# A recurrent memory layer on Trainium2: the query and key images of every segment transposed by DMA instead of on TensorE

## The chip, the cores and the metric

The kernel runs on one core of a Trainium2 chip. The core has a matrix engine (TensorE, PE), three engines that work on vectors (VectorE or DVE, ScalarE or ACT, GpSimd or POOL), and SyncE (SP), which in this kernel only issues DMA transfers. The engines run in parallel, each through its own list of instructions in order, and wait for each other by semaphores. The metric is the device time of one execution in microseconds (us), as the median of the runs shown.

## The reference

The model has four layers with a residual connection around each: A, B, A, B. Layer A is attention over segments of 32 rows with a recurrent memory of 8 rows; layer B is linear attention. The change touches layer A alone. Cut to what matters:

```python
x = x + A(layernorm(x)); x = x + B(layernorm(x)); x = x + A(layernorm(x)); x = x + B(layernorm(x))

def A(x, mem0, Wq, Wk, Wv, Wo, seg_len):          # x 2048x512, 64 segments of 32 rows, memory 8x512
    for s in range(64):
        h = concat(mem, x[32*s : 32*s+32])        # 40 rows
        q, k, v = h @ Wq, h @ Wk, h @ Wv          # 32 heads of 128
        p = softmax(mask(q @ k.T * 128**-0.5))    # memory columns are open, the rest is causal
        o = (p @ v) @ Wo                          # 40 x 512
        mem = o[:8]                               # the next segment's memory
        outs.append(o[8:])
    return concat(outs)
```

All weights and activations are bfloat16. The memory makes the 64 segments of a layer a recurrence: a segment's projections can't start until the output projection of the segment before has given the 8 memory rows.

## The kernel before

Each segment has 40 rows, but the kernel's matrix tiles take 32. Rows 0 to 31 of a segment (8 memory rows and 24 of its own) make its block; the 8 rows left over from each of four segments are put together into a left-over block of 32 rows per group of four segments (`prepare` and `left_block`, lines 671 to 706). The left-over block doesn't depend on the memory, and its projections are made ahead of time.

A projection (`project`, line 633) holds the 32 rows as weights in one of four column tiles of TensorE (`tile_position=(0, 32 * j)`) and streams 512 columns of Wq, Wk or Wv; four tiles j work side by side, so that a PSUM bank gets heads 8j + 4b to 8j + 4b + 3 of half b in its partitions 32j to 32j+31. That takes 16 products of 512 columns. A segment needs six: query and key for half 0, query and key for half 1, and the values for both halves (lines 888 to 895).

The scores need the query and key with the 128 elements of a head on the partitions, so the bank is copied to SBUF as a bfloat16 "image" of 128 x 512 (line 650, done by ScalarE or VectorE through the helper `evac`, lines 516 and 517) and then transposed. This is done in two ways before the change. `transposed` (lines 645 to 660) does it for a segment's own block: four 128 x 128 transposes on TensorE into PSUM (line 655), and a second copy from there to `qT` or `kT` (line 658). `turned` (lines 662 to 669) does it for the left-over block: one DMA transpose, issued by SP, from the image straight to its place (line 668).

With these, `mem_attention` (line 708) attends for the 8 memory rows: a bias product (717), scores (725), exponential (732), sums (737), reciprocal by logarithm and exponential (740, 742), values (750, 751) and the multiplication into `oTb` (754). `out_block` (832) does the output projection (823), and `next_mem` (836) picks the 8 rows out of it (842) and puts them into the next segment's block. `x_attention` (759) attends for the segment's other 32 rows, 24 of its block and 8 left over: lines 768 to 776 first copy the left-over query columns next to the segment's own, then multiply 32 columns of queries by each head's keys (774), again on four column tiles. Its values are at 807 and 808. Its result goes into the output projection of the next segment, so it isn't on the recurrence. `residual` (851) adds the outputs to x.

The order of the instructions is made by a planner (`_Prog.schedule`, lines 125 to 313). It is a list scheduler: every operation has a cost, written at its `add`; the longest path behind it gives its priority; and it is appended to its engine's list when the engine is free and its inputs are done. The cost of a DMA issue is 0.1 us on SP, and `lat` is the time from there to landing. Each engine then runs its list in this fixed order, whatever the real times are. `urgent` operations, those on the recurrence, may take the last PSUM banks. PE has two modes, `col` with four column tiles and `full`, and the planner groups work by mode. SP's list has the DMA transposes in the order of their planned starts, and an issue that waits for its image holds up those behind it.

Of the kernel before, what the change touches and what calls it, by code (L numbers as in the profile page):

```python
# [33 lines left out]
def c_pe(n_mm, n):  # L34
    return n_mm * max(0.0255, (n / 2.4 + 3.0) * 1e-3)
# [364 lines left out]
def _build_kernel(nc, A_x, A_mem0, A_Wq, A_Wk, A_Wv, A_Wo, A_seg_len, B_wqkv, B_wo, out):  # L400
# [11 lines left out]
    ANY = ("act", "dve")  # L412
# [54 lines left out]
    img = av((NI + 2) * 512).rearrange("p (r x) -> p r x", r=NI + 2)  # L467
    vimg = av(2 * 1024).rearrange("p (r x) -> p r x", r=2)
    vleft = av(2 * 1024).rearrange("p (r x) -> p r x", r=2)
    qT = av(2 * 1280).rearrange("p (r h j x) -> p r h j x", r=2, h=8, j=4)  # L470
    kT = av(2 * 1024).rearrange("p (r h j x) -> p r h j x", r=2, h=8, j=4)
    qTl = av(2 * 1024).rearrange("p (r h j x) -> p r h j x", r=2, h=8, j=4)
    kTl = av(2 * 1024).rearrange("p (r h j x) -> p r h j x", r=2, h=8, j=4)
# [155 lines left out]
    def a_layer(layer):  # L629
# [12 lines left out]
                add("pe", mm, c_pe4(4, 512), reads=[key] + bkeys, tiles=[tl], urgent=urgent, mode="col")  # L642
            return tl

        def transposed(W, key, blk, bkeys, b, dst, dkey, urgent):

            tl = project(W, key, blk, bkeys, b, urgent)
            k = img_no[0] % NI if urgent else NI + img_no[1] % 2
            img_no[0 if urgent else 1] += 1
            nd = evac(img[:, k, :], lambda: tl.f32()[:, :], 512, tiles=[tl], writes=[("img", k)], urgent=urgent)  # L650
            tt = P.tile()

            def tr(pe):
                for i in range(4):
                    r = pe.transpose(tt.bf16()[:, 128 * i:128 * i + 128], img[:, k, 128 * i:128 * i + 128], id_sb[:, :])  # L655
                return r
            add("pe", tr, c_pe(4, 128), reads=[("img", k), "id"], tiles=[tt], urgent=urgent)
            evac(dst, lambda: tt.bf16()[:, 0:512].rearrange("p (h j x) -> p h j x", h=4, j=4), 512, tiles=[tt],
                 writes=[dkey], rate=2, urgent=urgent)
            return nd  # L660

        def turned(W, key, blk, bkeys, b, dst, dkey):

            tl = project(W, key, blk, bkeys, b, False)
            k = NI + img_no[1] % 2
            img_no[1] += 1
            evac(img[:, k, :], lambda: tl.f32()[:, :], 512, tiles=[tl], writes=[("img", k)])
            add("sp", lambda e: e.dma_start_transpose(dst.rearrange("p h j x -> p h (j x)"), img[:, k, :]), 0.1,
                reads=[("img", k)], writes=[dkey], dsem="turn%d" % k, lat=3.0)

        def left_block(G):
            r2 = G % 2
# [86 lines left out]
        def x_attention(s):  # L759

            G, g = divmod(s, 4)
            r2, g2 = s % 2, G % 2
            s1 = (s + 1) % 3
            gl = slice(8 * g, 8 * g + 8)
            tl = P.tile()
            for b in range(2):
                hs = slice(4 * b, 4 * b + 4)
                add(ANY, copy(qT[:, r2, hs, :, 32:40], qTl[:, g2, hs, :, gl]),
                    {"act": c_act(128, 0, 1), "dve": c_dve(128)}, reads=[("qTl", g2, b)], writes=[("qTL", r2, b)])

                def mm(pe, b=b):
                    for hh in range(4 * b, 4 * b + 4):
                        for j in range(4):
                            r = pe.matmul(tl.f32()[32 * j:32 * j + 32, 32 * hh:32 * hh + 32], kT[:, r2, hh, j, :],  # L774
                                          qT[:, r2, hh, j, 8:40], start=True, stop=True, tile_position=(0, 32 * j))
                    return r
                add("pe", mm, c_pe4(16, 32), reads=[("kT", r2, b), ("qT", r2, b), ("qTL", r2, b)], tiles=[tl], mode="col")
            add("act", lambda a: a.activation(Px[:, :, :].rearrange("p h q -> p (h q)"), tl.f32()[:, 0:256], ACTF.Exp,  # L778
                                              scale=SCALE), c_act(256), tiles=[tl], writes=["Px"])
            add("dve", lambda v: v.tensor_tensor(Px[:, :, :], Px[:, :, :],  # L780
                                                 mx_sb[:, :].unsqueeze(1).to_broadcast([128, 8, 32]), ALU.mult),
                c_dve(256, 2), reads=["Px", "mx"], writes=["Px"])

            def sums(pe):
                o = tl.f32()[:, 256:512].rearrange("p (h q) -> p h q", h=8)
                pe.matmul(o, bo_sb[:, :], Px[:, :, :], start=True, stop=False)
                return pe.matmul(o[:, :, 24:32], bo_sb[:, :], PLL[:, g2, :, gl], start=False, stop=True)
            add("pe", sums, c_pe(1, 256) + c_pe(1, 64), reads=["Px", ("PLL", g2), "bo"], tiles=[tl])
            add("act", lambda a: a.activation(Rx[:, :, :].rearrange("p h q -> p (h q)"), tl.f32()[:, 256:512], ACTF.Ln),
                c_act(256), tiles=[tl], writes=["Rx"])  # L790
            add("act", lambda a: a.activation(Rx[:, :, :], Rx[:, :, :], ACTF.Exp, scale=-1.0), c_act(256, 0, 1),  # L791
                reads=["Rx"], writes=["Rx"])
            for j in range(4):
                q = slice(32 * j, 32 * j + 32)
                add("dve", lambda v, q=q, j=j: v.tensor_tensor(Pbx[q, :, j, 0:32], Px[q, :, :], Rx[q, :, :], ALU.mult),  # L795
                    c_dve(256), reads=["Px", "Rx"], writes=[("Pbx", j)])
                add("dve", lambda v, q=q, j=j: v.tensor_tensor(Pbx[q, :, j, 32:40], PLL[q, g2, :, gl], Rx[q, :, 24:32],  # L797
                                                               ALU.mult),
                    c_dve(64), reads=[("PLL", g2), "Rx"], writes=[("Pbx", j)])
            for b in range(2):  # L800
                pv = P.tile()
                for i in range(4):
                    def pvx(pe, i=i, b=b, pv=pv):
                        hh = 4 * b + i
                        o = pv.f32()[:, 128 * i:128 * i + 128].rearrange("p (j q) -> p j q", j=4)
                        e = slice(128 * hh, 128 * hh + 128)
                        pe.matmul(o, vimg[:, r2, e], Pbx[:, hh, :, 0:32], start=True, stop=False)  # L807
# [74 lines left out]
        for s in range(NSEG):  # L882
            G, g = divmod(s, 4)
            r2 = s % 2
            blk = hT[:, G % 2, g, :, :]
            bk = [("hTm", G % 2, g), ("hTx", G % 2, g)]
            early = []
            for b in range(2):
                hs = slice(4 * b, 4 * b + 4)
                transposed(Wq_sb, "Wq", blk, bk, b, qT[:, r2, hs, :, 0:32], ("qT", r2, b), True)  # L890
                early.append(transposed(Wk_sb, "Wk", blk, bk, b, kT[:, r2, hs, :, :], ("kT", r2, b), True))
            for b in range(2):
                tl = project(Wv_sb, "Wv", blk, bk, b, True)
# [174 lines left out]
```

## Time and profile before

| | before |
|---|---|
| median of 3 runs | 2032.45 us (2032.11 to 2033.56) |
| the profiled execution's own time | 2032.45 us |
| its span, first to last instruction | 2030.7 us |
| PE, ACT, DVE busy | 1946.7, 1274.8, 1015.3 us |
| granted clock of TensorE, mean | 0.988 |
| first memory layer's stretch, 63 to 935 us: PE busy | 864.46 of 872.00 us |
| second memory layer's stretch, 1070 to 1940 us: PE busy | 861.35 of 870.00 us |
| DMA transposes | 128, median 2.5 us from issue to landing |

The profile is one execution, recorded by the hardware. Busy time is the time in which an engine worked on an instruction; for PE it comes from modelled ends of pipelined products, so that "busy" isn't "at its peak". The chain of work that ended last is followed back from the last instruction, at each step to what released it, and tells which engine and line the time goes to. A group of instructions has a line number of the kernel; the copies of the helper `evac` all have its lines (516 on ACT, 517 on DVE) and are told apart by their shapes. Rows in order of time have the start, the duration, the engine, the line, what is written and read, and a count; what stands in brackets is the engine's idle time ahead of it and what ended it. "SPq" is SP's queue of DMA issues; its duration is the time for which the issue holds SP, and the landing is when the transfer's semaphore has its full count.

### The profile page before, as it was taken

What the parts mean: (1) busy time and instruction counts of PE and PEld (TensorE: products, weight loads), DVE (VectorE), ACT (ScalarE), POOL (GpSimd) and SP (SyncE); (2) the same over time, 40 slices, a digit from 0 to 9 for tenths busy, and PEclk for the clock granted to TensorE, in tenths of its full rate; (3) what the DMA queues carried; (4) which work ended last, traced back from release to release, by engine and by line L of the source; (5) the groups of instructions that cost most, each with busy time, mean ns of one, the idle gap of its engine ahead of it and who ended that gap; (6) DMA issues with size and microseconds to landing.
All of it is one profiled execution on the core that took longest, in us unless ns stands there. A gap on an engine that the chain in (4) does not pass through costs nothing.

```text
span 2030.7 us, 81374 instructions
## 1 busy us (share of the span) xinstructions
PE 1946.7 (96%) x37214; PEld 1150.5 (57%) x37214; DVE 1015.3 (50%) x3068; ACT 1274.8 (63%) x3203; POOL 23.6 (1%) x88
## 2 busy tenths in 40 slices
PE   2999999999999999997989999999999999999988
PEld 0555556555555555554645555555556555555555
DVE  0544444544444444445865444444444444444578
ACT  1666666666666666665646666666666666666654
POOL 3000000000000000000010000000000000000000
PEclk8999999999999999998999999999999999999989
DMA  9100000000000000001010000000000000000011
GB/s 362 34 10 13 10 13 11 12 10 13 13 11 13 13 14 10 13 8 43 1 15 16 8 13 11 13 13 13 10 13 13 10 11 13 13 10 13 5 42 43
DMA packets 82184, 47.17 MB, mean 23 GB/s; under 512 B 70056, under 2 KB 79280, under 8 KB 80304
## 3 DMA queue, kind: packets, MB, share of 16 engines
q1 hardware_dynamic: 81840, 41.97, 9.0%
q8 instruction: 291, 4.77, 1.0%
q14 instruction: 53, 0.43, 0.1%
HBM read 23.08 MB, written 2.10 MB: 12 GB/s over the span
## 4 chain that ended last, share of the span: by engine, by line
PE 93%; DMA 2%; DVE 2%; ACT 1%; issue 0%; SPq 0%; DVEq 0%
PE pb L639 43%; PE pb L823 15%; PE pb L655 6%; PE pb L842 3%; PE pb L807 3%; PE pb L944 3%; PE pb L725 3%; PE pb L857 2%; PE pb L737 2%; DMA Wv_sb<-in_A_Wv_dram 2%; PE pb L717 2%; PE pb L774 2%; PE pb L1011 1%; PE pb L937 1%; PE pb L750 1%; PE pb L751 1%
## 5 line engine op out<-in xcount | busy, mean ns | idle before, releaser
L516 ACT ACTIVATE arena_sb<-pb 128x512 bf16<-128x512 f32 (+6 forms) x1535 | 796.0, 523 | 421.9 <-PE pb L639 275.7
L639 PE MATMUL pb<-Wk_sb,arena_sb 128*32 128x512 bf16 x5120 | 353.3, 384 | 0.8 <-ACT arena_sb L516 0.8
L823 PE MATMUL pb<-Wo_sb,arena_sb 128*32 128x512 bf16 x5184 | 337.1, 384 | 8.7 <-DVE arena_sb L754 8.3
L639 PE MATMUL pb<-Wq_sb,arena_sb 128*32 128x512 bf16 x5120 | 344.4, 383 | 0.5 <-ACT arena_sb L516 0.5
L517 DVE COPY arena_sb<-pb 128x512 bf16<-128x512 bf16 (+2 forms) x474 | 178.5, 405 | 311.1 <-PE pb L655 307.4
L639 PE MATMUL pb<-Wv_sb,arena_sb 128*32 128x512 bf16 x5120 | 323.5, 380 | 0.5 <-DMA Wv_sb<-in_A_Wv_dram 0.5
L795 DVE TENSOR_TENSOR arena_sb<-arena_sb 32x256 bf16<-32x256 bf16 x512 | 213.3, 417 | 162.5 <-ACT arena_sb L791 150.6
L517 DVE CAST arena_sb<-pb 128x128 bf16<-128x128 f32 (+3 forms) x357 | 132.7, 375 | 179.6 <-PE pb L808 64.0
L639 PEld LDWEIGHTS pb<-Wk_sb,arena_sb 128*32 128x32 bf16 x5120 | 132.9, 97 | 126.9 <-issue 5.1
L639 PEld LDWEIGHTS pb<-Wq_sb,arena_sb 128*32 128x32 bf16 x5120 | 127.2, 97 | 130.7 <-ACT arena_sb L516 7.6
L639 PEld LDWEIGHTS pb<-Wv_sb,arena_sb 128*32 128x32 bf16 x5120 | 130.6, 96 | 121.7 <-DMA Wv_sb<-in_A_Wv_dram 0.6
L823 PEld LDWEIGHTS pb<-Wo_sb,arena_sb 128*32 128x32 bf16 x5184 | 122.1, 96 | 120.8 <-issue 11.3
L516 ACT ACTIVATE outW_sb<-pb 128x256 fp32r<-128x256 f32 x155 | 59.3, 382 | 184.8 <-PE pb L823 184.7
L655 PE MATMUL pb<-id_sb,arena_sb 128*128 128x128 bf16 x2048 | 157.3, 219 | 0.0
L655 PEld LDWEIGHTS pb<-id_sb,arena_sb 128*128 128x128 bf16 x2048 | 122.6, 97 | 55.4 <-ACT arena_sb L516 54.4
L807 PE MATMUL pb<-arena_sb 128*128 128x128 bf16 x1024 | 125.0, 217 | 4.1 <-DVE arena_sb L797 4.1
L797 DVE TENSOR_TENSOR arena_sb<-arena_sb 32x64 bf16<-32x64 bf16 x512 | 111.1, 217 | 15.8
L808 PE MATMUL pb<-arena_sb 128*128 128x32 bf16 x1024 | 114.3, 178 | 0.0
L732 ACT ACTIVATE arena_sb<-pb 128x256 bf16<-128x256 f32 x256 | 92.4, 383 | 32.9 <-PE pb L725 27.2
L842 PEld LDWEIGHTS pb<-selm_sb,outW_sb 128*128 128x128 f32 x504 | 75.1, 188 | 64.8 <-ACT arena_sb L778 23.8
L725 PE MATMUL pb<-arena_sb 128*128 128x32 bf16 x2048 | 102.8, 177 | 0.0
L517 DVE CAST outW_sb<-pb 128x256 fp32r<-128x256 f32 x105 | 44.5, 424 | 106.5 <-ACT outW_sb L516 103.4
(106 smaller groups left out, 2314.0 us busy)
## 6 DMA issues: line engine op xcount, KB each, us to landing
Wk_sb<-in_A_Wk_dram SPq DMA_DIRECT2D x1, 4096.0 KB, 12.6
Wq_sb<-in_A_Wq_dram SPq DMA_DIRECT2D x1, 4096.0 KB, 22.7
Wv_sb<-in_A_Wv_dram SPq DMA_DIRECT2D x1, 4096.0 KB, 31.9
Wo_sb<-in_A_Wo_dram SPq DMA_DIRECT2D x1, 4096.0 KB, 43.8
arena_sb<-in_B_wqkv_dram SPq DMA_DIRECT2D x2, 1536.0 KB, 6.3
arena_sb<-arena_sb SPq DMA_TRANSPOSE x128, 2.5
out_dram<-x_sb SPq DMA_DIRECT2D x16, 128.0 KB, 1.7
x_sb<-in_A_x_dram SPq DMA_DIRECT2D x1, 1920.0 KB, 9.3
```

The lines of the kernel that those rows point to most:

```text
L516: return e.activation(o() if callable(o) else o, i() if callable(i) else i, ACTF.Copy)
L517: return e.tensor_copy(o() if callable(o) else o, i() if callable(i) else i)
L639: r = pe.matmul(tl.f32()[32 * j:32 * j + 32, 0:512], blk[:, c, :], W[:, c, o:o + 512], start=(c == 0), stop=(c == 3), tile_position=(0, 32 ...
L655: r = pe.transpose(tt.bf16()[:, 128 * i:128 * i + 128], img[:, k, 128 * i:128 * i + 128], id_sb[:, :])
L725: r = pe.matmul(tl.f32()[:, o:o + 32], kk[:, hh, :, :].rearrange("p j x -> p (j x)"), qT[:, r2, hh, :, 0:8], start=False, stop=True, skip_ ...
L732: add("act", lambda a: a.activation(Pm[:, k, :, :].rearrange("p a q -> p (a q)"), tl.f32()[:, 0:256], ACTF.Exp, scale=SCALE), c_act(256), ...
L795: add("dve", lambda v, q=q, j=j: v.tensor_tensor(Pbx[q, :, j, 0:32], Px[q, :, :], Rx[q, :, :], ALU.mult), c_dve(256), reads=["Px", "Rx"], ...
L797: add("dve", lambda v, q=q, j=j: v.tensor_tensor(Pbx[q, :, j, 32:40], PLL[q, g2, :, gl], Rx[q, :, 24:32], ALU.mult), c_dve(64), reads=[("P ...
L807: pe.matmul(o, vimg[:, r2, e], Pbx[:, hh, :, 0:32], start=True, stop=False)
L808: return pe.matmul(o[:, :, 24:32], vleft[:, g2, e], Pbx[:, hh, :, 32:40], start=False, stop=True)
L823: r = pe.matmul(tl.f32()[32 * j:32 * j + 32, :], oT[:, 4 * hh + j, :], Wo_sb[:, 8 * j + hh, :], start=(hh == 0), stop=(hh == 7), tile_posi ...
L842: r = pe.matmul(tl.f32()[:, 8 * c:8 * c + 8], outW[:, s % 3, 128 * c:128 * c + 128], selm_sb[:, :], start=True, stop=True)
```

## The change

All query and key images of the memory layers go the second way. `transposed` is gone; `turned` now also serves the segments' own blocks, with the `urgent` mark and the ring of four images that `transposed` had, and its `lat` is 2.5 instead of 3.0. So the four images of a segment, query and key for half 0 and half 1, are transposed by four DMA transposes on SP's queue, with the semaphores turn0 to turn3; turn4 and turn5 are those of the left-over block, as before.

[...]`qT` no longer has 8 spare columns for the left-over queries. `x_attention` therefore doesn't copy them any more; it multiplies each head's keys twice, once by the 24 query columns of the block and once by the 8 left-over ones where they lie.

```diff
-    qT = av(2 * 1280).rearrange("p (r h j x) -> p r h j x", r=2, h=8, j=4)
+    qT = av(2 * 1024).rearrange("p (r h j x) -> p r h j x", r=2, h=8, j=4)
...
-        def transposed(W, key, blk, bkeys, b, dst, dkey, urgent):
+        def turned(W, key, blk, bkeys, b, dst, dkey, urgent=False):

             tl = project(W, key, blk, bkeys, b, urgent)
             k = img_no[0] % NI if urgent else NI + img_no[1] % 2
             img_no[0 if urgent else 1] += 1
             nd = evac(img[:, k, :], lambda: tl.f32()[:, :], 512, tiles=[tl], writes=[("img", k)], urgent=urgent)
-            tt = P.tile()
-
-            def tr(pe):
-                for i in range(4):
-                    r = pe.transpose(tt.bf16()[:, 128 * i:128 * i + 128], img[:, k, 128 * i:128 * i + 128], id_sb[:, :])
-                return r
-            add("pe", tr, c_pe(4, 128), reads=[("img", k), "id"], tiles=[tt], urgent=urgent)
-            evac(dst, lambda: tt.bf16()[:, 0:512].rearrange("p (h j x) -> p h j x", h=4, j=4), 512, tiles=[tt],
-                 writes=[dkey], rate=2, urgent=urgent)
+            add("sp", lambda e: e.dma_start_transpose(dst.rearrange("p h j x -> p h (j x)"), img[:, k, :]), 0.1,
+                reads=[("img", k)], writes=[dkey], dsem="turn%d" % k, lat=2.5)
             return nd
-
-        def turned(W, key, blk, bkeys, b, dst, dkey):
...
-            add("sp", lambda e: e.dma_start_transpose(dst.rearrange("p h j x -> p h (j x)"), img[:, k, :]), 0.1,
-                reads=[("img", k)], writes=[dkey], dsem="turn%d" % k, lat=3.0)
...
-                add(ANY, copy(qT[:, r2, hs, :, 32:40], qTl[:, g2, hs, :, gl]),
-                    {"act": c_act(128, 0, 1), "dve": c_dve(128)}, reads=[("qTl", g2, b)], writes=[("qTL", r2, b)])
-
                 def mm(pe, b=b):
                     for hh in range(4 * b, 4 * b + 4):
                         for j in range(4):
-                            r = pe.matmul(tl.f32()[32 * j:32 * j + 32, 32 * hh:32 * hh + 32], kT[:, r2, hh, j, :],
-                                          qT[:, r2, hh, j, 8:40], start=True, stop=True, tile_position=(0, 32 * j))
+                            q = slice(32 * j, 32 * j + 32)
+                            pe.matmul(tl.f32()[q, 32 * hh:32 * hh + 24], kT[:, r2, hh, j, :], qT[:, r2, hh, j, 8:32],
+                                      start=True, stop=True, tile_position=(0, 32 * j))
+                            r = pe.matmul(tl.f32()[q, 32 * hh + 24:32 * hh + 32], kT[:, r2, hh, j, :],
+                                          qTl[:, g2, hh, j, gl], start=True, stop=True, tile_position=(0, 32 * j))
                     return r
-                add("pe", mm, c_pe4(16, 32), reads=[("kT", r2, b), ("qT", r2, b), ("qTL", r2, b)], tiles=[tl], mode="col")
+                add("pe", mm, 2 * c_pe4(16, 32), reads=[("kT", r2, b), ("qT", r2, b), ("qTl", g2, b)], tiles=[tl], mode="col")
...
-                transposed(Wq_sb, "Wq", blk, bk, b, qT[:, r2, hs, :, 0:32], ("qT", r2, b), True)
-                early.append(transposed(Wk_sb, "Wk", blk, bk, b, kT[:, r2, hs, :, :], ("kT", r2, b), True))
+                turned(Wq_sb, "Wq", blk, bk, b, qT[:, r2, hs, :, :], ("qT", r2, b), True)
+                early.append(turned(Wk_sb, "Wk", blk, bk, b, kT[:, r2, hs, :, :], ("kT", r2, b), True))
```

In the changed file the DMA transpose is at line 651, the bias product at 701, the memory scores at 709, the two products of a pair at 756 and 758; other lines move up by 16.

More of the change, by code (lines that the diff above doesn't have):

```diff
@@ L650, in transposed @@
             nd = evac(img[:, k, :], lambda: tl.f32()[:, :], 512, tiles=[tl], writes=[("img", k)], urgent=urgent)
-            tt = P.tile()
-            def tr(pe):
-                for i in range(4):
-                    r = pe.transpose(tt.bf16()[:, 128 * i:128 * i + 128], img[:, k, 128 * i:128 * i + 128], id_sb[:, :])
-                return r
-            add("pe", tr, c_pe(4, 128), reads=[("img", k), "id"], tiles=[tt], urgent=urgent)
-            evac(dst, lambda: tt.bf16()[:, 0:512].rearrange("p (h j x) -> p h j x", h=4, j=4), 512, tiles=[tt],
-                 writes=[dkey], rate=2, urgent=urgent)
-            return nd
-        def turned(W, key, blk, bkeys, b, dst, dkey):
[L664 to L668, printed above, removed]
-                reads=[("img", k)], writes=[dkey], dsem="turn%d" % k, lat=3.0)
+            add("sp", lambda e: e.dma_start_transpose(dst.rearrange("p h j x -> p h (j x)"), img[:, k, :]), 0.1,
+                reads=[("img", k)], writes=[dkey], dsem="turn%d" % k, lat=2.5)
+            return nd
         def left_block(G):
```

## The prediction

> **What bounds the kernel now.** I read the page's busy shares and its chain first, then four segments in the middle of the first memory layer as one stretch, then the order of time of one segment on TensorE (PE) and ScalarE (ACT), and last the DMA issues.
>
> ```profile
> PE 1946.7 (96%) x37214; PEld 1150.5 (57%) x37214; DVE 1015.3 (50%) x3068; ACT 1274.8 (63%) x3203; POOL 23.6 (1%) x88
> ...
> PE 93%; DMA 2%; DVE 2%; ACT 1%; issue 0%; SPq 0%; DVEq 0%
> ```
>
> PE is the chain for 93% of the span. The stretch from 395.6 to 451.7 us holds four segments, 14.0 us each, and PE has no hole in it; its chain by line and the PE time of line 774 alone follow.
>
> ```profile
> by line: PE pb L639 48.3%; PE pb L823 18.3%; PE pb L655 7.2%; PE pb L842 4.2%; PE pb L807 3.6%; PE pb L725 3.1%; PE pb L857 2.5%; PE pb L737 1.9%; PE pb L717 1.8%; PE pb L774 1.8%; PE pb L750 1.7%; PE pb L786 1.4%; PE pb L751 1.4%; PE pb L8
> ```
>
> L655, the transposes that go, is 7.2% of 56.1 us, or 1.01 us a segment; L774, the score products that are split, 1.8%, or 0.25 us. Now one segment: its six projections, and after them the first transposes and scores. The ACT rows are the copies of four projections to their images.
>
> ```profile
> 424.67 1.04 PE L639 MATMUL pb<-Wq_sb,arena_sb 128*32 128x512 bf16 x16
> 425.54 1.04 PE L639 MATMUL pb<-Wk_sb,arena_sb 128*32 128x512 bf16 x16
> ...
> 428.12 1.90 PE L639 MATMUL pb<-Wv_sb,arena_sb 128*32 128x512 bf16 x32
> 429.96 0.62 PE L655 MATMUL pb<-id_sb,arena_sb 128*128 128x128 bf16 x8
> ...
> 425.76 0.60 ACT L516 ACTIVATE arena_sb<-pb 128x512 bf16<-128x512 f32 x1 [0.18 <-PE pb L639]
> 426.62 0.60 ACT L516 ACTIVATE arena_sb<-pb 128x512 bf16<-128x512 f32 x1 [0.27 <-PE pb L639]
> 427.49 0.60 ACT L516 ACTIVATE arena_sb<-pb 128x512 bf16<-128x512 f32 x1 [0.27 <-PE pb L639]
> 428.35 0.60 ACT L516 ACTIVATE arena_sb<-pb 128x512 bf16<-128x512 f32 x1 [0.27 <-PE pb L639]
> ```
>
> The projections run back to back, 0.86 us each. The first image is done 1.69 us after the first projection starts (424.67 to 426.36), the next ones 0.86 us apart. PE comes to the scores only after 5.29 us, so some time for a transfer is there already. Last, the SyncE (SP) queue: its issues at the start, and the DMA transposes of the whole run.
>
> ```profile
> 42.47 0.51 SPq L528 DMA_DIRECT2D arena_sb<-in_A_mem_dram  x1
> 43.04 1.20 SPq L668 DMA_TRANSPOSE arena_sb<-arena_sb  x1
> 44.29 0.59 SPq L532 DMA_DIRECT2D x_sb<-in_A_x_dram  x1
> ...
> L668 SPq DMA_TRANSPOSE arena_sb<-arena_sb x128: 1189/1190/12458, 30.0 to 1879.0; - x128
> ...
> DMA to landing us min/median/max: 2.4/2.5/17.6
> ```
>
> An issue holds SP for 1.19 us, and the next starts 0.05 us later. The 122 transposes after the first six issue 0.03 us after their image's copy ends. Of these, 69 land within 2.6 us (mean 2.43) and 53 later (mean 3.73, up to 4.47). The packets tell why: each late one, as far as I looked (the first 54), has a packet of the instruction queue over its own, nearly always one of 16 KB that lasts 0.9 to 1.6 us.
>
> **What the Trainium skill says.** "DMA: Bandwidth & Descriptors", Anatomy of one DMA, gives a fixed cost of about 2.0 us whatever the size, for another issue path; here 128 KB land after 2.43, of which packets run from 1.17 to 2.09 us. "Runtime: NRT & Kernel Launch", Instruction fetch mechanics, says that each sequencer fetches its program through a DMA queue in blocks of 16 KB, 256 instructions; the page's 291 packets with 4.77 MB agree. It calls this mostly hidden, which holds for PE here but not for transfers beside it. "TensorEngine Tiling (Array Packing)", Key Properties, has different column tiles work in parallel; in the trace four products on four column tiles take 25 ns together (L774), while full-array products 32 wide start 25 ns apart one by one (L750). "TensorE: Matmul & The Clock Gate", Part 1, puts the window that lowers the clock at some 3.4 us of idleness; the waits below are shorter, so I keep the 1.00 granted in this stretch. Nothing in the trace shows PE holes of this kind.
>
> **The change part by part**, per segment, 128 segments in two memory layers.
>
> *Removed from PE:* 16 transposes (2048 in all): -1.01 us. The four copies out of PSUM behind them (512 in all, 0.42 us on VectorE, 0.60 on ACT) and two copies of left-over query columns (0.19 to 0.30 us) go too, and are worth nothing: neither engine is over 63% busy, PE's products hide them.
>
> *Added to PE:* line 774's 32 products become 64, each pair on one column tile with the same weights, 24 and 8 columns. No run shows two in a row on one tile. Lower bound: the rate of L774, 16 quads by 25 ns is 0.40 instead of 0.20, so +0.2. Upper bound: the second waits for its tile as L750's products wait for the array, 28 ns a pair, 32 pairs, 0.90, so +0.7. I take the middle, +0.45. Part of it falls where PE would wait for an exponential anyway (0.38 us on ACT and 0.2 of PE's pipeline).
>
> *Moved to SP:* four more transposes a segment on a queue with one. The build shows where PE waits for them. In three of four segments PE runs the six projections, a bias product, scores that wait for transfer 1 (query) and 2 (key), a bias, 10 value products of the segment before (L807), scores that wait for 3, six more products of L807 and sums and values of the first half, and scores that wait for 4. From the first projection's start, without waits: 5.29 + 0.11 = 5.40 for transfer 1; +0.10 = 5.50 for 2; +0.10 +0.11 +5 x 0.082 = 6.12 for 3; +0.10 +3 x 0.082 +0.11 +0.21 = 6.79 for 4.
>
> Arrivals: issue 1 at 1.69 + 0.03 = 1.72, and since each image is done 0.86 us after the last while SP needs 1.24, the others at 2.96, 4.20 and 5.44. Plus 2.44: landings at 4.16, 5.40, 6.64, 7.88. With 0.1 (an estimate) until PE moves: transfer 1 is early, 2 just in time, 3 is met at 6.74, a wait of 0.62; then 4 is reached at 7.41 and met at 7.98, another 0.57. Together 1.2 us. Behind the waiting scores stand, in PE's order, the pair products, the second half's sums and values, the output projection, the next memory, and so the next segment's projections: all of it is late, as PE had no holes to give. The planner put the scores there because its costs give an issue 0.1 us on SP and 2.5 us to land, all four at once. The fourth segment, with the left-over rows' six projections, has other work in between, but two more transposes on SP just ahead; I get the same 1.2 there (0.3, 0.4 and 0.5). Both ends: 0.9, 1.5.
>
> *Instruction blocks:* a late landing costs 3.73 - 2.43 = 1.3 us. PE fetches about 2.3 blocks a segment (291 over 128); by instruction count some 0.7 fall in the 5.4 us in which the four transfers are in flight. One that hits the fourth is paid in full, the third lands at 7.94 and, with the 0.67 of products behind it, costs 0.7, the second 0.1, the first nothing: 0.7 x (1.3 + 0.7 + 0.1) / 4 = 0.37. If each transfer is late as often as before, 53 in 122 = 0.43, it is 0.43 x 1.3 + 0.57 x 0.43 x 0.7 = 0.73. I take the middle, 0.55 (ends 0.2, if fewer fall there, and 0.75).
>
> *Sum:* -1.01 + 0.45 + 1.2 + 0.55 = +1.19 us a segment, by 128 = 152 us. At the start the first segment's images now wait on queues with the rest of x (9.3 us to land): +5, an estimate. The b layers are untouched. 2030.7 + 157 = 2188 of span; a run is 1.75 above its span (2032.45, the median, is the profiled run), so 2190 us.
>
> **Rivals.** *Issues overlap (faster):* if SP could pass four transposes on as the planner thinks, transfer 4 would land at 4.28 + 0.03 + 2.44 = 6.75 and nothing would wait: -1.01 + 0.45 = -0.56, 128 times, 1967 us. It decides once the fourth lands by about 7.2. The start's rows (43.04 + 1.20, then 44.29) speak against. *Clean landings:* the PE that waits fetches no blocks, and they fall in the dense products after transfer 4; +0.64 by 128 and the start, 2119 us. *Recurrence as bound:* late landings (0.75) and pairs (0.7) cost their upper ends, and the tail of memory attention finds too few products left to hide its 1 us of Ln, exponential and multiply (L740, L742, L754), an estimated 0.4; -1.01 + 0.7 + 1.2 + 0.75 + 0.4 = +2.04, by 128 and the start, 2299 us. Against: the order keeps output products in that place. *The transposes don't go:* the build has all 2048 gone, so no.
>
> **How the numbers follow.** The sum as worked 0.63, clean landings 0.16, recurrence 0.12, overlapping issues 0.07, and 0.02 that gains and waits cancel. The likeliest's own range is 2140 to 2250; with the other slower cases and the bounds of the pairs, 2090 to 2290. A difference of 0.2%, 4 us, is about what a measurement can tell from none. Faster 0.07, same 0.02, slower 0.91.
>
> **What would show it.** Holes on PE in front of the score products (L709 in the new file), ended by the DMA transposes, the larger ones at transfers 3 and 4, in sum 1.2 to 2 us a segment; transposes issued 1.24 us apart in fours; landings of 2.4 us, and of 3.5 to 4.5 with a 16 KB packet beside them; L756 and L758 together 0.4 to 0.9 us a segment; PE busy 90% or less. The prediction is wrong if issues stand closer than 1.19 us, if PE finds its images landed, or if the pairs cost over 1 us.

## The result, and the profile after

| | before | after |
|---|---|---|
| median of 4 runs | 2032.28 us | 2227.65 us (2222.83 to 2231.47) |
| ratio, 95% interval | | 1.0962 [1.0938, 1.0987] |
| span of the profiled execution | 2030.7 us | 2229.8 us |
| mean granted clock of TensorE | 0.988 | 0.968 |

The changed kernel is 9.6% slower: 195 us, where 158 was forecast. First the page of the changed kernel: busy shares, the chain that ended last by engine and by line, the two rows of the score products, and the DMA issues.

```profile
PE 1969.7 (88%) x39262; PEld 1086.9 (49%) x39262; DVE 863.7 (39%) x2508; ACT 1221.7 (55%) x2995; POOL 23.6 (1%) x88
...
PE 66%; DMA 25%; DVE 4%; ACT 3%; issue 1%; SPq 1%; DVEq 0%; ACTq 0%
...
L709 PE MATMUL pb<-arena_sb 128*128 128x32 bf16 x2048 | 125.4, 179 | 166.2 <-DMA arena_sb<-arena_sb 162.9
...
arena_sb<-arena_sb SPq DMA_TRANSPOSE x640, 2.5
```

DMA was 2% of the chain and is 25%. PE is busy for 88% of the span instead of 96%, and its idle time stands in front of L709, the memory rows' scores: 166.2 us, of which 162.9 ended by a transpose. A transpose still takes 2.5 us to land. The two memory layers, 965 and 970 us long now (us, then busy time of PE, PEld, DVE, ACT, POOL with counts, granted clock, DMA share, GB/s):

```profile
65.00:1030.00 965.00, 875.16 (x18415) 476.97 (x18407) 346.99 (x1040) 545.70 (x1341) 0.00 (x0) 0.98 0.25 45
1170.00:2140.00 970.00, 872.41 (x18180) 475.67 (x18172) 340.01 (x1019) 543.61 (x1338) 0.21 (x2) 0.97 0.26 44
```

PE has 90 and 98 us without work in them, where it had 8 and 9, and the clock isn't full any more. The issues of the transposes, with the time for which one holds SP, and who waited for the landing:

```profile
L651 SPq DMA_TRANSPOSE arena_sb<-arena_sb x640: 1188/1264/2734, 40.0 to 2122.9; - x160
...
who waited for it (us, times):
  PEld pb L709: 217.2, 296
  PE pb L709: 162.9, 253
```

And one segment in order of time, from its values' projection on:

```profile
424.53 1.90 PE L639 MATMUL pb<-Wv_sb,arena_sb 128*32 128x512 bf16 x32
426.36 0.28 PE L701 MATMUL pb<-arena_sb,u_sb 128*128 128x256 bf16 x1
426.48 0.26 PE L709 MATMUL pb<-arena_sb 128*128 128x32 bf16 x4
426.89 0.26 PE L709 MATMUL pb<-arena_sb 128*128 128x32 bf16 x4 [0.16 <-DMA arena_sb<-arena_sb]
...
428.19 0.26 PE L709 MATMUL pb<-arena_sb 128*128 128x32 bf16 x4 [0.51 <-DMA arena_sb<-arena_sb]
...
429.48 0.27 PE L709 MATMUL pb<-arena_sb 128*128 128x32 bf16 x4
```

The first transfer is early, the second makes PE wait 0.16 us, the third 0.51 us. Ahead of the fourth, PE has nothing but four products of a left-over projection between 428.94 and 429.48. The order of the waits is the forecast one.

**Where the 195 us are.** I took the times from start to start of PE's products in both memory layers, from the first product of a layer that picks the next memory (L842 before, L826 after) to the last one, so that both kernels have the same 124 segments between the ends. What is usual for a pair of neighbouring products (the median of the same pair at the same place in its group of four; in front of the memory rows' scores, most of which wait, the lowest tenth) I call ordinary. What is more than 0.06 us longer is a wait, or, in a stretch with the clock at half, a loss to the clock. "Changes of mode", below, are steps between products on four column tiles and products on the full array.

| us, 124 segments | before | after | difference | per segment |
|---|---|---|---|---|
| ordinary steps | 1700.9 | 1662.7 | -38.2 | -0.31 |
| waits in front of the memory rows' scores | 0.9 | 185.3 | +184.4 | +1.49 |
| other waits | 17.3 | 23.8 | +6.5 | +0.05 |
| loss to the clock | 0 | 41.4 | +41.4 | +0.33 |
| sum | 1719.2 | 1913.2 | +194.0 | +1.56 |

By 128 segments that is 200 us; the profiled spans differ by 199.1. Where a wait lies partly in a stretch at half clock, its share is a matter of choice: up to 8 us move between the waits at the scores and the clock (185 to 193, 36 to 44).

### The profile page after: what moved, and what is told of

Same layout as the page of the kernel before. It is cut to its first block, busy times and chain, and to the rows that moved or that the text cites. A ratio compares the mean times of both kernels' runs of the same rounds, so it can differ in the third digit from the quotient of the medians.

```text
span 2229.8 us, 85170 instructions
## 1 busy us (share of the span) xinstructions
PE 1969.7 (88%) x39262; PEld 1086.9 (49%) x39262; DVE 863.7 (39%) x2508; ACT 1221.7 (55%) x2995; POOL 23.6 (1%) x88
## 4 chain that ended last, share of the span: by engine, by line
PE 66%; DMA 25%; DVE 4%; ACT 3%; issue 1%; SPq 1%; DVEq 0%; ACTq 0%
PE pb L639 31%; DMA arena_sb<-arena_sb 23%; PE pb L807 13%; PE pb L928 3%; PE pb L826 3%; PE pb L756 2%; ACT arena_sb L516 2%; PE pb L709 2%; DVE arena_sb L779 2%; DMA arena_sb<-in_A_mem_dram 2%; PE pb L841 2%; PE pb L721 1%; PE pb L995 1%; PE pb L921 1%; PE pb L791 1%
## 5 line engine op out<-in xcount | busy, mean ns | idle before, releaser
L516 ACT ACTIVATE arena_sb<-pb 128x512 bf16<-128x512 f32 (+6 forms) x1380 | 711.1, 519 | 477.7 <-PE pb L639 344.4
L517 DVE CAST arena_sb<-pb 128x128 bf16<-128x128 f32 (+3 forms) x376 | 158.8, 428 | 668.9 <-PE pb L792 323.2
L807 PE MATMUL pb<-Wo_sb,arena_sb 128*32 128x512 bf16 x5184 | 367.5, 407 | 3.3 <-DVE arena_sb L738 2.6
L639 PE MATMUL pb<-Wq_sb,arena_sb 128*32 128x512 bf16 x5120 | 353.8, 383 | 1.0 <-ACT arena_sb L516 0.5
L709 PE MATMUL pb<-arena_sb 128*128 128x32 bf16 x2048 | 125.4, 179 | 166.2 <-DMA arena_sb<-arena_sb 162.9
L709 PEld LDWEIGHTS pb<-arena_sb 128*128 128x128 bf16 x2048 | 89.0, 97 | 230.0 <-DMA arena_sb<-arena_sb 217.2
L807 PEld LDWEIGHTS pb<-Wo_sb,arena_sb 128*32 128x32 bf16 x5184 | 127.4, 100 | 134.9 <-issue 29.3
L516 ACT ACTIVATE outW_sb<-pb 128x256 fp32r<-128x256 f32 x196 | 75.3, 384 | 139.4 <-PE pb L807 137.3
L738 DVE TENSOR_TENSOR arena_sb<-pb,arena_sb 128x128 bf16<-128x128 f32 x256 | 74.5, 291 | 197.8 <-ACT arena_sb L726 97.9
L791 PE MATMUL pb<-arena_sb 128*128 128x128 bf16 x1024 | 142.1, 219 | 6.7 <-DVE arena_sb L781 6.4
L724 ACT ACTIVATE arena_sb<-pb 128x128 f32<-128x128 f32 x256 | 70.6, 276 | 126.5 <-PE pb L721 125.9
L792 PE MATMUL pb<-arena_sb 128*128 128x32 bf16 x1024 | 125.1, 179 | 0.0
L791 PEld LDWEIGHTS pb<-arena_sb 128*128 128x128 bf16 x1024 | 91.4, 97 | 39.0 <-issue 22.1
L826 PEld LDWEIGHTS pb<-selm_sb,outW_sb 128*128 128x128 f32 x504 | 73.3, 189 | 52.1 <-ACT outW_sb L516 21.6
```

What stands on the lines that cost most here:

```text
L516: return e.activation(o() if callable(o) else o, i() if callable(i) else i, ACTF.Copy)
L517: return e.tensor_copy(o() if callable(o) else o, i() if callable(i) else i)
L639: r = pe.matmul(tl.f32()[32 * j:32 * j + 32, 0:512], blk[:, c, :], W[:, c, o:o + 512], start=(c == 0), stop=(c == 3), tile_position=(0, 32 ...
L709: r = pe.matmul(tl.f32()[:, o:o + 32], kk[:, hh, :, :].rearrange("p j x -> p (j x)"), qT[:, r2, hh, :, 0:8], start=False, stop=True, skip_ ...
L738: add("dve", lambda v: v.tensor_tensor(oTb[:, s % 3, 16 * b:16 * b + 16, 0:8], pv.f32()[:, 0:128].rearrange("p (n q) -> p n q", q=8), Rm[: ...
L807: r = pe.matmul(tl.f32()[32 * j:32 * j + 32, :], oT[:, 4 * hh + j, :], Wo_sb[:, 8 * j + hh, :], start=(hh == 0), stop=(hh == 7), tile_posi ...
```

## The experiments

My theory after the result was: the transfers themselves cost nothing; what costs is that PE stands, in its fixed order, before scores whose images come late. In dispute was why they stand there: because the planner believes in 0.1 us for an issue (then better costs would mend it), or because the recurrence has nothing else to fill the time (then only an earlier landing helps). Ratios are to the kernel before, run on the same chip, with 95% intervals.

**The score pairs alone.** The kernel before, with line 774's products in two parts and without the copies of the left-over query columns:

```diff
-    r = pe.matmul(..., kT[:, r2, hh, j, :], qT[:, r2, hh, j, 8:40], ...)
+    pe.matmul(...[..., 0:24], kT[:, r2, hh, j, :], qT[:, r2, hh, j, 8:32], ...)
+    r = pe.matmul(...[..., 24:32], kT[:, r2, hh, j, :], qTl[:, g2, hh, j, gl], ...)
```

> The kernel before, with its TensorE transposes kept and only the score products of the x rows split into pairs of 24 and 8 columns. The profile after has the 64 products at 8 ns each, 0.51 us a segment instead of 0.25. If that is all the pairs cost: +0.26 x 128 = 33 us, some 10 us less since the planner's list has 96 fewer changes of mode, so about 2055 us. If two products on one column tile in a row really held each other up as the prediction's upper bound had it: +0.7 x 128, 2120 us.

Measured: 2063.39 us, 1.0154 [1.0138, 1.0169]: 32 us, or 0.25 a segment. A product in a pair starts 8 ns after the one before it, hardly more than in the row of 32 columns (7.4 ns); so 64 products cost twice what 32 cost. The 10 us that fewer changes of mode were to give back aren't seen, though there are 96 fewer (1132 instead of 1228). Of the 195 us, 32 have nothing to do with DMA.

**The transfers without anyone who waits.** The kernel of the last experiment, with TensorE's transposes kept, and in addition the changed kernel's four DMA transposes a segment, written to a place that nothing reads:

```diff
+    add("sp", lambda e: e.dma_start_transpose(spare[:, k % 2, :, :], img[:, k, :]), 0.1,
+        reads=[("img", k)], writes=[("spare", k % 2)], dsem="spare%d" % (k % 2), lat=2.5)
```

> The kernel with pairs and TensorE transposes, and besides, each of a segment's four images also transposed by DMA to a place that nothing reads: the same SP issues and the same traffic as in the changed kernel, but only the image's next user waits for them. Theory: 2063 us as without them, within 15. Rival (the traffic slows engines, copies or the fetch of instructions): 2090 us or more.

Measured: 2063.71 us, 1.016 [1.0145, 1.0175], the same as without them. The chain that ended last:

```profile
PE 93%; DMA 3%; DVE 2%; ACT 1%; issue 1%; SPq 0%
```

All 640 transposes run, and DMA is 3% of the chain. So neither the traffic nor SP's time costs anything by itself: the loss to DMA comes from the consumers that wait.

**The costs of an issue put right.** The changed kernel, with the planner told that an issue takes 1.25 us on SP:

```diff
-    ... img[:, k, :]), 0.1, reads=[("img", k)], writes=[dkey], dsem="turn%d" % k, lat=2.5)
+    ... img[:, k, :]), 1.25, reads=[("img", k)], writes=[dkey], dsem="turn%d" % k, lat=1.25)
```

> The changed kernel, with only the planner's figures for a DMA transpose altered: 1.25 us on SP and landing 1.25 us after that, in place of 0.1 and 2.5. The program does the same work; only the order differs. Theory (the scores stand too early in PE's list since the planner lets SP issue all four at once): the waits at the scores fall from 1.37 us a segment to some 0.4, which late landings cost, and with them most dips of the clock; 110 more changes of mode cost 11 us; about 2110 us. Rival (the late landings through instruction blocks are the bulk): waits stay over 1 us a segment, over 2180 us.

Measured: 2245.62 us, 1.1062 [1.1034, 1.1091]: no gain, rather a small loss against the changed kernel. The chain of waits tells where the time went.

```profile
PE pb L709 <- DMA arena_sb<-arena_sb: 102.0, 111, 2.4
...
PE pb L770 <- DVE arena_sb L764: 14.7, 17, 1.8
PE pb L721 <- ACT arena_sb L716: 12.9, 69, 0.4
PE pb L807 <- DVE arena_sb L738: 12.6, 24, 1.6
```

PE waits 102.0 us at L709 instead of 162.9, but new waits have come up behind the scores, for the exponential (L721) and for the memory rows' result (L807), so that PE's idle time between the ends of the layers (gaps over 0.15 us) falls only from 177 to 163 us. This list also has 1542 changes of mode, 110 more; at the 0.1 to 0.26 us that one costs (see below) they are worth 11 to 29 us, about what was gained.

**The landing put later still.** The same with a longer time to land, so that the planner allows for late landings too:

```diff
-    ... img[:, k, :]), 0.1, reads=[("img", k)], writes=[dkey], dsem="turn%d" % k, lat=2.5)
+    ... img[:, k, :]), 1.25, reads=[("img", k)], writes=[dkey], dsem="turn%d" % k, lat=2.6)
```

> As the run before, but with landing 2.6 us after the 1.25 on SP, so that the planner places the scores as if every transfer was late through an instruction block. Theory of both causes: waits fall to some 0.1 to 0.2 us a segment and the clock stays up, but 400 more changes of mode than in the changed kernel cost 40 us; about 2090 us. If late landings don't matter, it is no better than the run before, or worse by 20 to 30 us.

Measured: 2380.16 us, 1.1706 [1.1675, 1.1736], the slowest of all.

```profile
PE pb L807 <- DVE arena_sb L738: 96.6, 158, 1.2
PE pb L721 <- ACT arena_sb L716: 58.6, 131, 0.8
...
PE pb L709 <- DMA arena_sb<-arena_sb: 32.0, 51, 1.6
```

The scores hardly wait any more, 32.0 us. The products that the planner has put ahead of them are those that used to cover the tail of memory attention; there PE now waits 96.6 and 58.6 us. PE's idle time is 214 us, the clock, at 0.929, costs 108 us instead of 41, and 1836 changes of mode, 404 more, come on top. So the theory of wrong costs falls for these two lists: each moved the hole and closed little or none of it. That no other order could do better isn't shown; the halves below show that order matters.

**The recurrence loosened.** To see whether the recurrence is what can't be filled, each kernel gets its memory rows from the segment two before (the output is another function of the inputs, from the same work; both first segments get the start memory):

```diff
-    G1, g1 = divmod(s + 1, 4)
+    G1, g1 = divmod(s + 2, 4)
...
-    if s + 1 < NSEG:
+    if s + 2 < NSEG:
```

> The changed kernel with the recurrence loosened: a segment takes the memory rows of the segment two before it (the first two take the start memory), so its output is another function; the work and the DMA transposes are the same, 128 segments with four each. The planner now has two segments to mix. New theory (the recurrence itself, lengthened by the transfers, is the bound, and no order of the list can hide it): the waits at the scores almost go, the clock stays up, and the time falls to PE's work, 1664 us of the layers and 303 around them plus some changes of mode, 1980 to 2010 us, below the kernel before. Rival (SP's issues, the DMA traffic or the late landings cost by themselves): it stays above 2130 us.

> The kernel before with the same loosened recurrence (memory rows of the segment two before). PE had no holes, so there is nothing to gain but small waits: 2000 to 2030 us. If it falls as far as the changed kernel does, the recurrence was a bound before as well and the pair says nothing on the transfers.

Measured: the changed kernel goes to 2074.33 us, 1.0208 [1.019, 1.0227], which is 153 less; the kernel before to 1969.78, 0.9696 [0.9682, 0.9711], 62 less. Both miss their ranges: the changed kernel stays above the kernel before, which falls further than small waits would explain. A looser recurrence is worth 91 us more to the changed kernel, but not all of that is latency of the transfers. By the same count as above, for 128 segments, its waits at the scores fall by 52 us and its ordinary steps by 91 (in the kernel before by 46): with two segments to mix, the planner's lists change mode only 628 times instead of 1432 (before: 808 instead of 1228). So of the gap of 195, half at most, and by the waits about a quarter, is latency that the recurrence keeps PE from filling. The rest stays: in the changed kernel PE still waits at the scores, though there is another segment's work.

```profile
PE pb L709 <- DMA arena_sb<-arena_sb: 115.5, 130, 2.6
```

Its list has a fixed order, made for transfers that land together. I take this for the second half of the mechanism, since it is there without the recurrence; a run with the looser recurrence and better costs, which would show it, I didn't make.

**An earlier last landing.** Query and key image of a half in one transpose of 128 x 1024, two issues a segment instead of four:

```diff
-    turned(Wq_sb, "Wq", blk, bk, b, qT[:, r2, hs, :, :], ("qT", r2, b), True)
-    early.append(turned(Wk_sb, "Wk", blk, bk, b, kT[:, r2, hs, :, :], ("kT", r2, b), True))
+    for W, key in ((Wq_sb, "Wq"), (Wk_sb, "Wk")):
+        tl = project(W, key, blk, bk, b, True)
...
+        nd = evac(img[:, k, :], lambda tl=tl: tl.f32()[:, :], 512, tiles=[tl], writes=[("img", k)], urgent=True)
+    early.append(nd)
+    add("sp", lambda e, dst=dst, k=k: e.dma_start_transpose(dst.rearrange("p a h j x -> p (a h) (j x)"),
+        img[:, k - 1:k + 1, :].rearrange("p a x -> p (a x)")), 0.1, ..., lat=2.5)
```

> The changed kernel with the query and key image of a half moved by one DMA transpose of 128 x 1024, two issues a segment instead of four. If an issue holds SP for 1.2 us whatever its size, the second half is issued at 4.31 us and lands some 7.6 us after the first projection, 0.3 earlier than now, and the time falls by 0.3 x 128, to 2190 us. If SP's time grows with the size, to 2.4 us, the second half lands at about 9 us, and by the theory of the recurrence the time grows by some 1 us a segment, to 2350 us.

Measured: 2073.14 us, 1.0207 [1.0184, 1.0229], 155 less than the changed kernel. The row of these issues, then the chain of waits:

```profile
L879 SPq DMA_TRANSPOSE arena_sb<-arena_sb x256: 1230/1232/2354, 52.8 to 1961.0; - x128
...
DMA to landing us min/median/max: 3.0/3.1/4.8
```

```profile
PE pb L708 <- DMA arena_sb<-arena_sb: 58.9, 77, 1.9
```

Twice the data hold SP for 1.23 us, against 1.19, and land after 3.1 us, against 2.5. So SP's time is per issue, whatever its size here, and the kernel is faster than I had expected even for that case. In the changed kernel, the fourth image lands 8.8 us after the first projection starts, in the mean of all segments (issue 1 at 1.8, 4.2 for the three issues ahead of the fourth, 2.73 to landing); here the second transpose lands at 7.7 (issue at 4.45, 3.26 to landing). That is 1.1 us a segment, 140 us. The waits at the scores fall by 130 us (185.3 to 55.5) and the loss to the clock by 31 (41.4 to 10.0); 155 were found.

**Which half goes by DMA.** The changed kernel with one half's images transposed by DMA and the other's on TensorE (the mirror image of this has `b == 1`):

```diff
+    way = turned if b == 0 else transposed
+    way(Wq_sb, "Wq", blk, bk, b, qT[:, r2, hs, :, :], ("qT", r2, b), True)
```

> The changed kernel with the query and key images of half 0 transposed by DMA and those of half 1 on TensorE; pairs as in the changed kernel. Two transfers a segment, on the two images that are done first: issues at 1.72 and 2.96 us, landings at 4.16 and 5.40, before the projections end. Theory (only the last image's arrival lengthens the recurrence): 2063 us of the kernel with pairs and TensorE transposes, less 8 transposes, 0.5 x 128 = 64, and 10 us of waits back: 2000 to 2020 us. Rival (each transfer in a segment costs, wherever it stands): half of the 165 us that lie between that kernel and the changed one, 2140 us.

> The mirror of the run before: half 1 by DMA, half 0 on TensorE. The same numbers of transfers, transposes and products. Issues at 3.44 and 4.68 us, landings at 5.9 and 7.1 when nothing is late, 8.4 when a block hits the last; with the products of the tail behind. Theory: the last image is again the one that is waited for, 0.4 to 0.8 us a segment, so 50 to 100 us slower than the run before, 2060 to 2110 us. Rival: the two are equal within 10 us.

Measured: half 0 by DMA 2097.67 us, 1.0308 [1.0284, 1.0332]; half 1 by DMA 2043.16, 1.0049 [1.0034, 1.0064]. The opposite of what I expected. Half 0's chain of waits, and PE in one of its segments:

```profile
PE pb L726 <- DMA arena_sb<-arena_sb: 48.9, 61, 1.9
```

```profile
442.37 0.28 PE L718 MATMUL pb<-arena_sb,u_sb 128*128 128x256 bf16 x1
442.54 0.27 PE L726 MATMUL pb<-arena_sb 128*128 128x32 bf16 x4
443.25 0.27 PE L726 MATMUL pb<-arena_sb 128*128 128x32 bf16 x4 [0.44 <-DMA arena_sb<-arena_sb]
443.36 0.61 PE L655 MATMUL pb<-id_sb,arena_sb 128*128 128x128 bf16 x8
```

The scores that wait (L726) stand ahead of half 1's transposes (L655), whose images have long been there. PE reaches them 5.4 us after the first projection starts, just when the key's transfer lands at best, so that each late landing holds up the eight transposes and all that follows. Now the chain of waits with half 1 by DMA, and one of its segments:

```profile
PE pb L726 <- DMA arena_sb<-arena_sb: 14.3, 22, 1.3
```

```profile
439.98 1.05 PE L639 MATMUL pb<-Wq_sb,arena_sb 128*32 128x512 bf16 x16
...
441.70 1.19 SPq L668 DMA_TRANSPOSE arena_sb<-arena_sb  x1
442.94 1.26 SPq L668 DMA_TRANSPOSE arena_sb<-arena_sb  x1
...
445.28 0.62 PE L655 MATMUL pb<-id_sb,arena_sb 128*128 128x128 bf16 x8
...
446.33 0.27 PE L726 MATMUL pb<-arena_sb 128*128 128x32 bf16 x4
```

The issues come 1.72 and 2.96 us after the first projection starts, not at 3.44 and 4.68: the planner projects the half that goes by DMA first, here as with half 0, and in every one of the 128 segments (medians of the issues 1.71 and 2.96 us in both kernels). So this pair doesn't compare early with late images, as I had meant; it compares the places of the scores. With half 1 by DMA, the other half's transposes, and in about half of the segments its scores too, stand ahead of the scores that wait. PE comes to its first scores after 6.26 us (median) instead of 5.42, and most late landings fall into that work. By the count above, the 124 segments take 1785.7 and 1729.0 us. Of the 57 us between them, the waits at L726 make 42 (62.3 against 19.9), the clock 5 and the ordinary steps 13, while other waits give 3 back. The 62 changes of mode that half 0 has more are worth 6 to 16 of the 13 (0.1 to 0.26 us each, see below).

**The best use of the DMA.** Three kernels made from the one before, all with 32-column scores (no pairs), the queries transposed on TensorE and the keys by DMA. First with two issues:

```diff
-    early.append(transposed(Wk_sb, "Wk", blk, bk, b, kT[:, r2, hs, :, :], ("kT", r2, b), True))
+    early.append(turned(Wk_sb, "Wk", blk, bk, b, kT[:, r2, hs, :, :], ("kT", r2, b), True))
```

> The kernel before, with only the two key images of a segment transposed by DMA; queries stay on TensorE, their left-over columns are copied, there are no pairs. The planner's list has the two key projections first, then the queries, then the values. Theory: images done at 1.69 and 2.55 us after the first projection, issues at 1.72 and 2.96, landings at 4.16 and 5.40; the scores that need them stand after 5.3 us of projections and 0.5 us of query transposes, so even a landing late by 1.3 us is nearly hidden. 8 transposes go, -0.5 x 128 = -64 us, waits give back 10 to 20: about 1985 us, faster than both. Rival (a DMA in the recurrence costs a wait wherever it stands): 0.6 us a segment of waits or more, 2040 us or slower.

Measured: 2026.66 us, 0.9975 [0.9963, 0.9987], from 2015.53 to 2034.06 in 19 runs. That is a gain of a quarter of a percent, where I expected 2.3%. In the profiled execution (2017.82) the ordinary steps are 38 us shorter, but the waits 18 longer, and the clock costs 6; the waits are in front of the left-over block's scores (L689, 10 us, where the kernel before had 1), whose transfers share the queue, and of the product that picks the next memory (L843, 18 us, before 1). What makes PE wait at L843 stays open. Then with the keys projected first and both key images in one transpose:

```diff
+    for b in range(2):
+        tl = project(Wk_sb, "Wk", blk, bk, b, True)
+        early.append(evac(img[:, b, :], lambda tl=tl: tl.f32()[:, :], 512, tiles=[tl], writes=[("img", b)], urgent=True))
+    add("sp", lambda e, r2=r2: e.dma_start_transpose(kT[:, r2, :, :, :]..., img[:, 0:2, :]...), 0.1, ..., lat=3.1)
     for b in range(2):
         transposed(Wq_sb, "Wq", blk, bk, b, qT[:, r2, hs, :, 0:32], ("qT", r2, b), True)
```

> The kernel with only the keys by DMA, and both key images of a segment in one transpose of 128 x 1024: issue at 2.6 us, landing 3.06 later at 5.65, about the time that the projections end and before the scores need it; a late one at 6.9 just touches them. Theory: SP has one issue less and the left-over block's transfers wait less, 2005 to 2020 us, faster than the kernel before and than the run with two issues (2027). Rival (the waits of that run come from elsewhere): 2025 to 2035 us.

Measured: 1999.24 us, 0.9833 [0.9819, 0.9848], 34 us faster than the kernel before, and a little below the range expected. Its chain that ended last, its DMA issues and its chain of waits:

```profile
PE 82%; DMA 9%; DVE 4%; ACT 3%; issue 1%; SPq 1%; DVEq 0%
...
arena_sb<-arena_sb SPq DMA_TRANSPOSE x256, 3.1
```

```profile
PE pb L725 <- DMA arena_sb<-arena_sb: 9.6, 18, 0.9
```

PE does 8 transposes a segment less and waits 9.6 us in all for the keys, since their 3.1 us of flight are covered by the two query projections and what follows them. Of all kernels here with the reference's recurrence this is the fastest. Last, the same with the left-over block's four transposes merged into two:

```diff
+    for W, key, dst, dk in ((Wq_sb, "Wq", qTl, "qTl"), (Wk_sb, "Wk", kTl, "kTl")):
...
+        add("sp", lambda e, dst=dst: e.dma_start_transpose(dst[:, r2, :, :, :]..., img[:, NI:NI + 2, :]...), 0.1, ..., lat=3.1)
```

> As the run before, and the left-over block's four transposes merged into two (both query images, both key images). The waits of its scores for their transfers were 12 us with two issues of keys; theory: they stay or shrink a little, 2000 to 2020 us. If merging delays the left-over images more than it saves on SP, some 10 us slower than the run before.

Measured: 2006.68 us, 0.9878 [0.9861, 0.9894], 7 us slower than without. A merged issue has to wait for its second image, and the left-over block isn't on the recurrence; which wait makes the 7 us I didn't find out.

## Why the prediction was right, and where it was off

Direction and range were right, and so was the mechanism, PE standing before scores whose transposes SP issues one by one; 2190 was 38 us short. That it came so near is in part luck: two terms were too large, by 0.45 us a segment together, and three that were put at nothing make some 0.6. By its own steps, per segment:

| step | forecast | measured |
|---|---|---|
| transposes removed | -1.01 | -1.01 (their time before; all 2048 are gone) |
| score pairs | +0.45 (0.2 to 0.7) | +0.25 (alone), +0.26 in the changed kernel |
| waits at the scores, clean and late landings | 1.2 + 0.55 = 1.75 | 1.49 |
| other waits | 0 | +0.05 |
| changes of mode | 0 | about +0.2 |
| clock | 0 | +0.33 |
| not assigned | | about +0.25 |
| sum | +1.19 | +1.56 |

*The pairs.* The middle of the bounds was wrong: the lower end, the rate of L774 itself, is what the chip does. Nothing shows a product waiting for its own column tile.

*The waits.* SP's spacing was the right key: the fourth transfer is the latest, and of the time that the four scores of a segment wait, the first in PE's order has 7%, the others 22, 37 and 34%. The size of 1.75 was too large by 0.26. With the waits taken out, PE comes to the four scores at 5.41, 5.52, 6.15 and 7.21 us (medians), so the way to the fourth is 0.4 us longer than the 6.79 of the forecast. The landings were off the other way: issues in a row start 1.31 us apart in the median, not 1.24, and one can hold SP for up to 2.7 us. 180 of 634 transfers landed late (mean 3.61 us, the others 2.48), which is 28% where my upper end took 43%. From 1 us after the issue to landing, 161 of the 180 have a 16 KB instruction packet beside them, of the other 454 only 49. The forecast's 2.3 blocks a segment count the b layers' products too; 34599 of PE's 37214 lie in the stretches of the two layers, which makes 2.1.

*The changes of mode.* Not in the forecast. With other work put between the scores, PE goes from column tiles to the full array and back more often: 1432 changes instead of 1228. From a 512-column product on a column tile to a full-array one it takes 0.31 us, start to start, where the next column product starts after 0.05; there are 39 more of these (10 us), 63 more from a narrow column product to the full array and 102 more back, at about 0.1 us (17 us).

*The clock.* I wrote that the single waits are shorter than the window of 3.4 us that the Trainium skill gives in "TensorE: Matmul & The Clock Gate", Part 1, and kept 1.00. The trace has that window: the clock falls to half in 27 places of the two layers, mostly for 3.41 us each. But no step from one product to the next was longer than 2.6 us there, and each of the ten longest (2.1 to 2.6 us) has such a fall at its end or within 2.4 us behind it. So a wait need not fill a window to cost the clock; what share of it must be idle, no run shows.

*The start.* Of the +5 us little is seen: the first product that picks the next memory comes at 66.8 us instead of 63.6, and about 1.6 of these 3.1 us are what every segment has.

*The cause.* Why the scores stand there was only half right. The prediction blamed the planner's 0.1 us for an issue. Two kernels with better costs were slower: by the waits that came up at L721 and L807, the products that would fill the hole are the same that hide the tail behind it. The rival with the recurrence as bound said this ("finds too few products left"), at too high a price for pairs and late landings. (Among the rivals, the sum with overlapping issues comes to 1966, not 1967; nothing hangs on it.) What the runs support is both of its sides: a shorter way to the last image pays about microsecond for microsecond (merged issues, one run: 1.1 us less, 1.2 gained), and a looser recurrence pays 91 us more than in the kernel before, some half of it in waits at the scores. What they add is that a wait's place in PE's list counts as much as its length, as the two halves show.

*Late landings.* The Trainium skill, "Runtime: NRT & Kernel Launch", Instruction fetch mechanics, calls the block fetches mostly hidden. For transfers beside them the trace again says otherwise: the late ones, nine in ten of them beside such a block, take 3.61 us instead of 2.48.

## What to carry to other kernels

In these kernels an operand that goes by DMA did best where it was made first, went in one issue, and was met in the consumer's list behind work that was ready. On a recurrence, count issue plus flight for the last operand, and subtract only work that isn't needed to hide something else. Before you read a pair of runs, look where the planner put the work: a change of costs or of ways can reorder more than you meant. Take a doubtful transfer apart from its consumer (the same transfer, unread) before you blame the queue.

## What was not expected of the hardware

- An issue of a DMA transpose holds SP for 1.19 us with 128 x 512 elements and for 1.23 us with 128 x 1024; the landing goes from 2.5 to 3.1 us.
- The clock went to half for 3.41 us and more, with no step between products longer than 2.6 us, 41 us in all; with more and shorter waits (late costs put in) it fell to 0.929, 108 us.
- The kernel before, with hardly a hole in PE, gained 62 us from the looser recurrence: its ordinary steps shrank by 46 us, with 420 fewer changes of mode. Part of what looks like a full PE is the spacing that the order forces.
